# Splitting the last 96 rows of a weight matrix over two queues and both ends of a decode kernel

## The chip, the cores and the metric

One core of one Trainium2 chip. The metric is the device time of one execution in microseconds (us), as a median of several. Before: 659.82 us (3 runs, 659.73 to 659.85).

## The reference, cut to what matters

```python
h  = x  + attention(layernorm(x), k_cache, v_cache, wq, wo)   # B=2, one new token, 32 heads, 8192 keys, Dh=128
h2 = h  + (relu(ln @ W_gate) * (ln @ W_up)) @ W_down          # ln = layernorm(h), D=512, F=1376
```

K and V are 2 x 32 x 8192 x 128 bf16 each, 268 MB together. All else is small: wq and wo 4 MB each, the three matrices of the second part 1.4 MB each. W_down has 1376 = 10 x 128 + 96 rows; the last 96 rows, 1 KB each, are the subject.

## The kernel before

SyncE issues nearly every load. The start, and the places that matter at the end (cuts marked):

```python
nc.scalar.dma_start(x_row, A_x[:, 0]).then_inc(sem_x, 16)
nc.sync.dma_start(slot[3][:], A_wq.rearrange("(p c) n -> p (c n)", c=DC)).then_inc(sem_wq, 16)
nc.sync.dma_start(wo_rows, ...).then_inc(sem_wl, 16)
load(0, A_k_cache, 0); load(1, A_v_cache, 0); load(2, A_k_cache, 1)
# ... 32 pairs of K and V tiles of 4 MB through four slots ...
# last tiles in flight: the weights of the second part, into slot 0
for k, w in enumerate((B_W_up, B_W_gate)): nc.sync.dma_start(slot[0][...], w...)
for k, (r0, n) in enumerate(((0, 4), (4, 4), (8, 2))):              # three blocks of W_down
    nc.sync.dma_start(slot[0][...], B_W_down[r0 * 128:(r0 + n) * 128]...).then_inc(sem_wd[k], 16)
nc.sync.dma_start(wd_last[:], B_W_down[F - FR:]).then_inc(sem_wd[3], 16)   # FR = 96
# ... up product, gate product, hd = relu(gate) * up, then the down product:
order = [(f, k) for k, (r0, n) in enumerate(WD_BLOCKS) for f in range(r0, r0 + n)] + [(10, 3)]
for n, (f, k) in enumerate(order):
    pe.wait((sem_wd[k], 16))
    for m in range(4): nc.tensor.matmul(Op[0][...], lhsT=hd[...], rhs=...)
```

So the 96 rows are the last load issued and the last operand used.

The softmax here doesn't subtract the row's maximum and nothing guards it: scores larger than these inputs give would overflow.

## Time and profile before

| | before |
|---|---|
| median | 659.82 us |
| span in the profile | 658.6 us |
| DMA's part of the chain that ended last | 80% |
| bytes read | 281 MB, 427 GB/s over the span |
| PE's wait for wq ends | 12.98 us |
| third block of W_down complete | 656.09 us |
| the 96 rows complete | 656.29 us |

A load that is spread over all 16 DMA engines tells its arrival by 16 counts on a semaphore, one from each engine. The trace keeps the time of each, so a load has a first, a mean and a last arrival. The mean says how far the stream as a whole has come; the last says when a waiting engine may start. What PE waited for first:

```profile
12.98 0.10 PEld L256 LDWEIGHTS O<-slot,xlT 128*2 128x2 bf16 x8 [7.73 <-DMA slot<-in_A_wq_dram]
```

The brackets give the idle time before the instruction and what ended it: PE had been ready for 7.73 us, so wq's arrival sets the start of everything.

### The profile page before, as it was taken

Reading aid. Unit: us, or ns where it says so; the run is one execution under the profiler, and the core shown is the slowest. Engines: PE = TensorE matmul, PEld = TensorE weight load, DVE = VectorE, ACT = ScalarE, POOL = GpSimd, SP = SyncE. Lnnn points to the kernel's source line nnn. Section 1 sums busy time; section 2 is a strip of 40 time slices with the busy share of each in tenths; the row PEclk is TensorE's granted clock in tenths of the full one; section 3 lists DMA queues with packets and bytes.
Section 4 is the critical chain, followed back from the end, with each engine's and each line's share of the span. In section 5 each row is a group of like instructions: output and inputs, shape, how many; then the busy total and the mean of one; then the engine's idle time right before and its main releaser. Section 6 shows DMA issues by size and latency. Waiting matters only on the chain.

```text
span 658.6 us, 7569 instructions
## 1 busy us (share of the span) xinstructions
PE 326.1 (50%) x3066; PEld 192.1 (29%) x3067; DVE 469.4 (71%) x280; ACT 214.2 (33%) x433; POOL 72.7 (11%) x125
## 2 busy tenths in 40 slices
PE   2753444435554354644535453554445454454586
PEld 0431322214332132422213232322323222232354
DVE  1585576788767678776768867677876767787991
ACT  1622332243342233334223243323324322433151
POOL 3001002020200202020020201102020010202000
PEclk9999565565576555576655577555566755557567
DMA  8999999999999999999999999999999999999997
GB/s 366 445 426 437 426 442 418 442 420 444 424 436 438 422 440 420 444 422 438 430 432 438 422 440 420 444 422 438 440 422 436 424 438 424 440 428 436 434 415 307
DMA packets 10645, 281.17 MB, mean 427 GB/s; under 512 B 1190, under 2 KB 1292, under 8 KB 1804
## 3 DMA queue, kind: packets, MB, share of 16 engines
q1 hardware_dynamic: 10628, 281.06, 99.4%
q8 instruction: 5, 0.08, 0.0%
q14 instruction: 4, 0.03, 0.0%
q10 hardware_dynamic: 8, 0.00, 0.0%
HBM read 281.05 MB, written 0.00 MB: 427 GB/s over the span
## 4 chain that ended last, share of the span: by engine, by line
DMA 80%; DVE 18%; issue 1%; SPq 0%; DVEq 0%; PE 0%
DMA slot<-in_A_k_cache_dram 76%; DVE prod L539 16%; DMA slot<-in_B_W_down_dram 4%; DVE prod L548 2%; DVE scores L553 0%; SPq L171 0%; SPq L702 0%; SPq L698 0%; DVE kT L815 0%; DVEq L586 0%; PE O L807 0%; DVEq L590 0%; SPq L175 0%; SPq L174 0%; DVE zi L505 0%
## 5 line engine op out<-in xcount | busy, mean ns | idle before, releaser
L539 DVE TENSOR_TENSOR prod<-slot,q_c 128x12288 bf16<-128x12288 bf16 x32 | 209.9, 6558 | 148.1 <-DMA slot<-in_A_k_cache_dram 141.4
L404 PE MATMUL O<-slot,e 128*16 128x512 bf16 x1024 | 117.2, 609 | 219.3 <-ACT e L494 146.3
L548 DVE TENSOR_TENSOR prod<-prod 128x6144 bf16<-128x6144 bf16 (+3 forms) x128 | 212.3, 1658 | 7.8
L565 ACT ACTIVATE kT<-T 128x1024 bf16<-128x1024 bf16 x128 | 126.2, 1022 | 144.6 <-PE T L380 141.7
L380 PE MATMUL T<-ident_f,slot 128*128 128x128 f32 x512 | 112.8, 376 | 29.4 <-DVEq L586 29.4
L404 PEld LDWEIGHTS O<-slot,e 128*16 128x16 bf16 x1024 | 26.1, 112 | 284.6 <-ACT e L494 172.9
L494 ACT ACTIVATE e<-scores 64x96 bf16<-64x96 f32 x64 | 19.5, 304 | 239.8 <-DVEq L600 237.0
L380 PEld LDWEIGHTS T<-ident_f,slot 128*128 128x128 f32 x512 | 81.9, 193 | 44.4 <-DVEq L586 43.6
L536 POOL COPY q_c<-q_all 128x136 bf16<-128x136 bf16 x32 | 56.3, 1760 | 196.4 <-DVEq L590 152.5
L363 PE MATMUL S<-q_c,kT 128*128 128x4 bf16 x1024 | 47.6, 168 | 39.2 <-ACT kT L565 38.5
L363 PEld LDWEIGHTS S<-q_c,kT 128*128 128x128 bf16 x1024 | 39.6, 104 | 66.8 <-ACT kT L565 65.5
L416 PE MATMUL Ob<-sel,os_sb 128*128 128x4 f32 x136 | 31.0, 351 | 24.0 <-ACT os_sb L568 24.0
L416 PEld LDWEIGHTS Ob<-sel,os_sb 128*128 128x128 f32 x136 | 29.5, 319 | 25.9 <-ACT os_sb L568 25.9
L519 POOL MEMSET O_l<- 128x40 bf16 (+1 forms) x13 | 1.8, 136 | 303.9 <-DVEq L597 303.9
L553 DVE TENSOR_REDUCE scores<-prod 128x96 f32<-128x768 bf16 x32 | 30.5, 953 | 2.8
L565 ACT ACT_TABLE_LOAD x15 | 19.2, 1283 | 0.3
L494 ACT ACTIVATE e<-S 64x32 bf16<-64x32 f32 x64 | 13.0, 203 | 15.1 <-PE S L363 14.7
L568 ACT ACTIVATE os_sb<-O 128x512 f32<-128x512 f32 x17 | 10.2, 597 | 11.6 <-PE O L404 11.3
L494 ACT ACTIVATION_READ_ACCUMULATOR e<-S 64x1 f32 x64 | 12.8, 201 | 0.7
L494 ACT ACTIVATION_READ_ACCUMULATOR e<-scores 64x1 f32 x64 | 11.8, 184 | 0.0
L425 PEld LDWEIGHTS Ob<-zs,ones_f 128*128 128x128 f32 x30 | 7.1, 294 | 12.8 <-issue 12.8
L524 POOL COPY rsel<-rows 128x30 bf16<-128x30 bf16 x28 | 5.9, 209 | 33.3 <-DVEq L597 32.5
(104 smaller groups left out, 90.6 us busy)
## 6 DMA issues: line engine op xcount, KB each, us to landing
slot<-in_A_k_cache_dram SPq DMA_DIRECT2D x32, 4096.0 KB, 32.1
slot<-in_A_v_cache_dram SPq DMA_DIRECT2D x31, 4096.0 KB, 30.3
slot<-in_A_wq_dram SPq DMA_DIRECT2D x1, 4096.0 KB, 12.1
X<-in_A_wo_dram SPq DMA_DIRECT2D x1, 3840.0 KB, 46.0
slot<-in_A_v_cache_dram SPq DMA_DIRECT2D x1, 3072.0 KB, 23.1
slot<-in_B_W_up_dram SPq DMA_DIRECT2D x1, 1376.0 KB, 21.7
slot<-in_B_W_gate_dram SPq DMA_DIRECT2D x1, 1376.0 KB, 24.7
slot<-in_A_v_cache_dram SPq DMA_DIRECT2D x1, 1024.0 KB, 25.2
```

The lines of the kernel that those rows point to most:

```text
L363: i = nc.tensor.matmul(Sp[p % 2][:, 2 * jj:2 * jj + 4], lhsT=kv_[:, k, r, :], rhs=q_c[p % 2][:, 4 * r:4 * r + 4], start=(r == 0), stop=(r ...
L380: i = nc.tensor.transpose(Tp[g % 2][:, k * 128:(k + 1) * 128], k_t[:, j:j + 2, :].rearrange("p j d -> p (j d)").bitcast(F32), ident_f[:])
L404: i = nc.tensor.matmul(Op[0][c:c + 16, :], lhsT=e_t[q][:, j // VJ, :], rhs=v_t[:, j:j + VJ, :].rearrange("p j d -> p (j d)"), start=(q == ...
L416: i = nc.tensor.matmul(Ob[:, 0:4], lhsT=os_sb[:, jj * Dh:(jj + 1) * Dh], rhs=sel[:, 4 * jj:4 * jj + 4], start=(jj == 0), stop=(jj == VJ - 1))
L425: return nc.tensor.matmul(bank[:, ZC:ZC + 8], lhsT=ones_f[:], rhs=zs[:], start=True, stop=True)
L494: i = nc.scalar.activation(out=e_t[q][h, j0 // VJ:j1 // VJ, 8 * q:8 * q + 8].rearrange("p g (j a) -> p g j a", a=2)[:, :, :, a], in_=src(h ...
L536: nc.gpsimd.tensor_copy(out=q_c[p % 2][:], in_=q_all[:, p]).then_inc(g2d, 1)
L539: return nc.vector.tensor_tensor(out=prod[:, 0:JC, :], in0=tile((2 * p) % 4)[:, 0:JC, :], in1=q_c[p % 2][:, 8:QW].unsqueeze(1).broadcast_t ...
L548: run(nc.vector.tensor_tensor(out=prod[:, 0:JC, 0:w], in0=prod[:, 0:JC, 0:w], in1=prod[:, 0:JC, w:2 * w], op=ALU.add))
L553: return nc.vector.tensor_reduce(out=scores[p % PG][:, 0:JC], in_=prod[:, 0:JC, 0:8], axis=AX.X, op=ALU.add)
L565: to_pe(nc.scalar.activation(out=kT[gg % 2][:], in_=Tp[gg % 2][:].bitcast(BF16), func=ACT.Copy))
L568: to_pe(nc.scalar.activation(out=os_sb[:], in_=Op[0][:], func=ACT.Copy))
```

## The change

The intent, as I read it: take the 96 rows out of the last place of SyncE's queue, put 28 of them into the first microseconds, where the DMA engines are still idle, and let GpSimd's own queue bring the other 68 while PE works on gate.

```diff
+    WD_TAIL = ((68, 16), (84, 12), (0, 68))
+                def load_tail(eng, k):
+                    r0, n = WD_TAIL[k]
+                    eng.dma_start(
+                        wd_last[r0:r0 + n], B_W_down[F - FR + r0:F - FR + r0 + n]).then_inc(sem_wd[3 + k], 16)
                 nc.scalar.dma_start(x_row, A_x[:, 0]).then_inc(sem_x, 16)
+                load_tail(nc.sync, 0)
+                load_tail(nc.gpsimd, 1)
                 nc.sync.dma_start(slot[3][:], A_wq.rearrange("(p c) n -> p (c n)", c=DC)).then_inc(sem_wq, 16)
...
-                        nc.sync.dma_start(wd_last[:], B_W_down[F - FR:]).then_inc(sem_wd[3], 16)
...
                 t_u = ffn_in(Sp[1], wup, 0, FC)
+                pool.wait(t_u)
+                load_tail(nc.gpsimd, 2)
...
-                    pe.wait((sem_wd[k], 16))
+                    for j in range(k, k + 1 if k < 3 else 6):
+                        pe.wait((sem_wd[j], 16))
```

More of the change, by code (lines that the diff above doesn't have):

```diff
@@ L98, in bass_sequential_preLN__gqa_block_cached__glu_gated_reglu__decode_kernel @@
         sem_w = [S(f"w{i}") for i in range(2)]
-        sem_wd = [S(f"wd{i}") for i in range(4)]
+        sem_wd = [S(f"wd{i}") for i in range(6)]
         slot = [sb(f"slot{i}", [128, SLOT], BF16) for i in range(4)]
```

## The prediction

> **What bounds the kernel now.** I read the page's queue table and 40 slices first, then the chain that ended last, then the order of instructions at both ends, and last the single DMA packets and arrivals, because the change touches only transfers.
>
> ```profile
> DMA  8999999999999999999999999999999999999997
> q1 hardware_dynamic: 10628, 281.06, 99.4%
> DMA 80%; DVE 18%; issue 1%; SPq 0%; DVEq 0%; PE 0%
> ```
>
> The 16 DMA engines are busy in every slice; only the first and the last are below nine tenths. The 18% of DVE on the chain is bookkeeping: it multiplies the K tile it has just received while the next tiles are already flowing. In the middle of the chain one loop trip takes 38.9 us (519.60 to 558.46 us) and brings four loads of 4096 KB, 16.78 MB: 432 GB/s. The bytes do not change here, so the time is **when the stream starts, plus the bytes at that rate, plus how raggedly the 16 engines finish.** I therefore look at the two ends. The start, SyncE's issues in order of time:
>
> ```profile
> 0.81 0.40 SPq L174 DMA_DIRECT2D slot<-in_A_wq_dram  x1
> 1.27 0.42 SPq L175 DMA_DIRECT2D prod<-in_A_wo_dram  x1
> 1.73 0.42 SPq L171 DMA_DIRECT2D slot<-in_A_k_cache_dram  x1
> ```
>
> One issue follows the other every 0.46 us. Among the packets, wq's first one begins at 1.83 us, 1.02 us after its issue began. Before that the engines carry only x. The end, first the stretches (the last two figures are the share of 16 engines busy, and GB/s), then the chain and the instructions:
>
> ```profile
> 653.00:654.00 1.00, 1.00 (x37) 1.00 (x35) 0.00 (x0) 0.00 (x0) 0.00 (x0) 0.50 0.95 356
> 654.00:655.00 1.00, 0.64 (x20) 0.56 (x20) 0.18 (x1) 0.00 (x0) 0.00 (x0) 0.50 0.42 148
> 655.00:656.00 1.00, 0.94 (x32) 0.37 (x20) 0.00 (x0) 0.00 (x0) 0.00 (x0) 0.50 0.22 74
> ...
> 629.40 26.68 DMA slot<-in_B_W_down_dram
> 656.09 0.04 issue
> 656.13 0.52 PE O L807 x7
> ...
> 656.13 0.38 PE L807 MATMUL O<-slot,hd 128*2 128x128 bf16 x8 [0.20 <-DMA slot<-in_B_W_down_dram]
> 656.34 0.28 PE L807 MATMUL O<-wd_last,hd 96*2 96x128 bf16 x4
> ```
>
> From 654 us most engines have nothing left, yet the kernel waits until 656.09 us for the **third block of W_down**, not for the last 96 rows. The arrivals show why. The first W_down block reaches its 16 counts in three flocks: eight at 652.10 to 652.27, three at 652.66 to 652.79, five at 653.47 to 653.91. Five engines run 1.4 to 1.8 us behind the leaders. The lag is old: after the second V load one engine is already about 1 us behind, just after an instruction fetch (a packet of 16,384 B at 32.49 us, 1.06 us long) ran on one engine; another such fetch at 57.56 us puts a second one behind. Because the queue never runs dry, nobody catches up. The third block's last count comes at 656.09 us, the 96 rows' last at 656.29 us. PE needs from 656.13 to 656.34 us to issue the eight matmuls of the third block, and only then wants the 96 rows: **their wait is hidden to within hundredths of a microsecond.**
>
> **What the Trainium skill says.** "DMA: Bandwidth & Descriptors", section "Issuing engines are not separate DMA queues": all queues share the same 16 engines, so issuing from GpSimd buys no bandwidth, only issue time. This trace has no GpSimd data transfer to test that with; it does show the engines shared (the instruction fetches of another queue delay data). The same page, section "Why a DMA increments its semaphore by 16 and not by 1": a transfer uses the largest number of engines up to 16 that divides its rows, so 16 rows use 16, 12 use 12 and 68 use 4, taken on GpSimd in turn from a round-robin cursor; but it also tells of GpSimd transfers spread by ceil(rows/16) per engine, which for 68 rows is 5 rows on 13 engines and 3 on one. The trace agrees for 96 rows (16 counts arrive); no run before shows 12 or 68. The same page, "Anatomy of one DMA — SWDGE (gpsimd) path": about 2 us fixed for a GpSimd transfer. Nothing before shows it. "Runtime: NRT & Kernel Launch", section "Instruction fetch mechanics": instructions are refilled in 16 KiB blocks; the 16,384 B packets agree.
>
> **The change part by part.**
>
> 1. *Sixteen rows by SyncE ahead of wq.* The data is nothing: one row of 1 KB per engine, 46 ns a packet in this trace. But wq's issue moves one period back, from 0.81 to 1.27 us, so its first packet comes at about 2.29 instead of 1.83 us. The row occupies 0.05 us of that; the rest is an empty engine. wq itself has slack nowhere, since everything queues behind it: **+0.46 us**, and it persists through the loop, because DMA is the bound.
> 2. *Twelve rows by GpSimd at the start.* At one row per engine, 0.04 us on twelve engines, within wq's stream or in the gap before it: **+0.0 to +0.04**. Its issue also delays GpSimd's constants by an estimated 1 to 2 us. The transposes that need them ran at 4.9 us, and PE then waited for wq until 12.98 us, 7.6 us: hidden.
> 3. *The 96 rows leave the end of SyncE's queue.* That is 6 rows, 6 x 46 ns = 0.28 us on every engine, and one issue of 0.50 us that ran at 630.2 us with over 20 us of work queued: hidden. The 0.28 us lie behind the third block in each engine's ring, so the third block's arrival does not move. Gain: 656.34 minus the end of the eight issues, **0 to -0.05**.
> 4. *68 rows by GpSimd after the up product.* Up ended at about 651.7 us, later by part 1. Adding the skill's 2 us as an estimate, the rows would be there near 654 to 655 us if alone, before the third block at 656.5. They matter only if they sit on a lagging engine ahead of its third block. On four leading engines: 17 x 46 ns = 0.78 us inside 1.7 us of idleness, **0**. On fourteen engines: 5 x 46 ns on the laggards too, **+0.21 to +0.23**. On four engines with a laggard among them: up to **+0.75**.
> 5. *Two more waits on PE* before the last four matmuls: an issue step on the chain is 0.02 to 0.1 us, **+0.0 to +0.1**, mostly under the eight matmuls.
>
> Sum of parts 1, 2 and 3 with four leading engines: 659.82 + 0.46 + 0.04 - 0.03 = 660.3. With the fourteen-engine spread 660.5; with a laggard hit 661.0.
>
> **The rivals.** *The front is free.* The first wq packets took 1.4 to 2.2 us against 1.22 us later, and all end at 3.7 to 4.05 us whether they began at 1.83 or 2.64. Something at the start is common to all and need not be the issue; if the small transfer takes that start-up upon itself, wq may lose nothing. Against it: x's packets at 1.75 us took only 44 ns, so the engines were not cold, and a fill delay would recur after an idle gap. Time 659.7 to 659.9. *The laggards gain.* If the kernel waited for the 96 rows, 0.28 us would come off, which is surely the intent: rows placed on engines that stand idle, and balanced as 12 and 4. The arrivals speak against it (656.09 rules, not 656.29). Time 659.5 without a front loss, and 660.0 with one. *GpSimd's transfer is late.* If issue plus landing takes over 4.5 us, the last 68 rows take over from the third block as the last wait; the skill's 2 us speak against it, contention in a shared ring for it. Time 661 or more. *Instruction fetches move.* Added instructions shift the 16 KiB boundaries; one fetch more or fewer on a laggard is 1 us on that engine: +-0.3 at most on average.
>
> **Range and chances.** I weigh the full front cost at about 6 in 10, a partly or fully hidden front at 3 in 10, and a fourteen-engine or laggard hit on top at about 4 in 10. The middle is 660.2 us; 659.5 to 660.9 covers both the intent coming true and a moderate hit. A 2% change is 13 us; nothing here is a tenth of that except a wholly unexpected stall of GpSimd. So 0.004 for faster, 0.988 for the same, 0.008 for slower.
>
> **What would show each step.** Right: wq's issue at 1.27 and its first packet near 2.29 us; PE's wait for wq ends near 13.4 instead of 12.98; K and V arrivals all about 0.46 us later; one-row GpSimd packets near 2 to 3 us; at the end the third block still the last wait, near 656.5, and the 68 rows landed before it. Wrong: K arrivals unchanged against before (front free); the flocks of arrivals changed in size or lag (rows on laggards, or moved fetches); PE's last wait on the 96-row tile; a GpSimd transfer that takes many microseconds, or holds up the first transposes past 12.98 us.

## The result, and the profile after

660.42 us (6 runs, 660.32 to 660.58) against 659.84 us (6 runs, 659.65 to 660.08) in the same rounds: 0.58 us longer. The ratio is 1.0009, with a 95% interval of 0.9996 to 1.0022. Ratios are the mean time of one kernel's fast runs over that of the other's of the same rounds, so not quite the ratio of the medians that I quote. Every one of the six runs is slower than every one of the six before, and a second measurement, with other kernels beside it, gave 660.34 (5 runs) against 659.90 (9 runs), again without overlap. The half microsecond is real, and small.

The changed kernel's start, in order of time:

```profile
0.82 0.39 SPq L176 DMA_DIRECT2D wd_last<-in_B_W_down_dram  x1
1.26 0.41 SPq L182 DMA_DIRECT2D slot<-in_A_wq_dram  x1
1.32 0.66 POOL L176 DMA_DIRECT2D wd_last<-in_B_W_down_dram  x1 [0.81 <-POOLq L851]
...
6.14 0.40 PE L249 MATMUL T<-ident,kT 2*128 2x2 bf16 x8 [6.14 <-DVE kT L240]
...
13.76 0.10 PEld L264 LDWEIGHTS O<-slot,xlT 128*2 128x2 bf16 x8 [7.31 <-DMA slot<-in_A_wq_dram]
```

wq is issued at 1.26 instead of 0.81 us, and PE starts on it at 13.76 instead of 12.98 us. GpSimd's issue, 0.66 us, delays the constants and with them the transposes to 6.14 us; PE still waits 7.31 us for wq after that, so this part is hidden.

The end of the chain, then PE's last groups:

```profile
630.18 26.46 DMA slot<-in_B_W_down_dram
656.65 0.04 issue
656.69 0.56 PE O L817 x10
...
656.69 0.10 PEld L817 LDWEIGHTS O<-slot,hd 128*2 128x2 bf16 x8 [0.34 <-DMA slot<-in_B_W_down_dram]
656.92 0.12 PEld L817 LDWEIGHTS O<-wd_last,hd 96*2 96x2 bf16 x4
```

The last wait is again for the third block (656.65, before 656.09), and the last four weight loads follow with no idle time of their own. The end has the same shape as before and is 0.56 us later. The three small loads and what they took from issue to landing (last column, us):

```profile
wd_last<-in_B_W_down_dram POOLq DMA_DIRECT2D x1, 68.0 KB, 4.0
wd_last<-in_B_W_down_dram SPq DMA_DIRECT2D x1, 16.0 KB, 1.7
wd_last<-in_B_W_down_dram POOLq DMA_DIRECT2D x1, 12.0 KB, 7.5
```

GpSimd's 12 rows take 7.5 us, although each of the packets takes 46 ns. The single packets show how. The rows were issued at 1.32 us, but are served only at 6.60 to 6.95 us, when each engine has served three packets of wq, 32 KB each. From there on an engine serves one 1 KB row, then a packet of wq (1.213 us), then GpSimd's 4-byte count, then the next packet of wq. The Trainium skill says in "DMA: Bandwidth & Descriptors", section "Queues, rings and completion order", that an engine takes turns between queues, a packet at a time. This trace agrees from the row on; why three packets of wq pass before it is not shown.

**Where the time comes from, in arrivals (us):**

| kernel | wq first packet | wq mean | V tile at 615 us, mean | third block, mean | third block, last |
|---|---|---|---|---|---|
| before | 1.83 | 12.79 | 615.38 | 654.81 | 656.09 |
| before_again | 1.83 | 12.79 | 615.38 | 654.83 | 655.81 |
| after | 2.30 | 13.37 | 615.96 | 655.37 | 656.65 |
| after_again | 2.30 | 13.34 | 615.92 | 655.33 | 656.51 |

The mean is 0.55 to 0.58 us late at wq, the first large load, and 0.50 to 0.56 us late at the last one. **By the arrivals the whole loss is made before 14 us and carried nearly unchanged through 640 us of full DMA queue.** Note how well the mean repeats (12.79 and 12.79) while the last arrival moves by 0.28 us between two runs of one kernel. For effects of this size the mean is the better instrument. It has its own chance, though, once something stands ahead of wq: in the two runs of one kernel under 1 and 2 below, wq's mean is 13.14 and 13.30.

The packets split the loss into parts. By the bytes that the large packets had moved, the changed kernel (two profiles) was 0.47 and 0.44 us late as soon as the first megabyte was in, before any row of GpSimd was served: that is SyncE's transfer ahead of wq. GpSimd's rows add 0.04 us where they are served. Another 0.07 us comes between 14 and 45 us, where the 32 KB packets take slightly longer than before (the arrivals show this part already at wq). Packets are longer there in all six profiles in which rows of a second queue were served among wq's packets, and in none of the other eight. Why is open.

### The profile page after: what moved, and what is told of

The parts are those of the page before. It is cut to its first block, busy times and chain, and to the rows that moved or that the text cites. A ratio compares the mean times of both kernels' runs of the same rounds, so it can differ in the third digit from the quotient of the medians.

```text
span 659.2 us, 7572 instructions
## 1 busy us (share of the span) xinstructions
PE 329.5 (50%) x3066; PEld 195.2 (30%) x3067; DVE 469.2 (71%) x280; ACT 214.4 (33%) x433; POOL 74.7 (11%) x127
## 4 chain that ended last, share of the span: by engine, by line
DMA 80%; DVE 18%; SPq 1%; issue 1%; DVEq 0%; PE 0%
DMA slot<-in_A_k_cache_dram 76%; DVE prod L547 16%; DMA slot<-in_B_W_down_dram 4%; DVE prod L556 2%; DVE scores L561 0%; SPq L172 0%; SPq L710 0%; SPq L706 0%; DVE kT L825 0%; PE O L817 0%; DVEq L594 0%; DVEq L598 0%; SPq L183 0%; SPq L182 0%; SPq L176 0%
## 5 line engine op out<-in xcount | busy, mean ns | idle before, releaser
L388 PE MATMUL T<-ident_f,slot 128*128 128x128 f32 x512 | 116.7, 386 | 29.2 <-DVEq L594 29.2
L388 PEld LDWEIGHTS T<-ident_f,slot 128*128 128x128 f32 x512 | 84.3, 198 | 44.3 <-DVEq L594 43.4
L502 ACT ACTIVATE e<-S 64x32 bf16<-64x32 f32 x64 | 12.9, 202 | 15.2 <-PE S L371 14.8
L502 ACT ACTIVATION_READ_ACCUMULATOR e<-S 64x1 f32 x64 | 12.8, 201 | 0.7
L433 PEld LDWEIGHTS Ob<-zs,ones_f 128*128 128x128 f32 x30 | 7.3, 303 | 12.8 <-issue 12.8
```

The source lines that it names most:

```text
L388: i = nc.tensor.transpose(Tp[g % 2][:, k * 128:(k + 1) * 128], k_t[:, j:j + 2, :].rearrange("p j d -> p (j d)").bitcast(F32), ident_f[:])
L433: return nc.tensor.matmul(bank[:, ZC:ZC + 8], lhsT=ones_f[:], rhs=zs[:], start=True, stop=True)
L502: i = nc.scalar.activation(out=e_t[q][h, j0 // VJ:j1 // VJ, 8 * q:8 * q + 8].rearrange("p g (j a) -> p g j a", a=2)[:, :, :, a], in_=src(h ...
```

## The experiments

Theory: SyncE's issue ahead of wq leaves the DMA engines without work for one issue period, and a full queue never gives it back; the end is neutral. Rivals: GpSimd's transfers make the loss; bytes make it, or a one-off start-up cost, and not the issue; the end part gains or loses. Times are medians of five runs, each beside the kernel before on the same chip. The interval of every ratio is about plus or minus 0.0013, 0.9 us, and holds 1.0 in all of them, so the verdicts rest on the arrivals, and on the medians only as a check. Edits are shown against the changed kernel (in e6_all_behind against the kernel before), cut to the lines that matter; the table of pieces and the waits follow them.

**1. SyncE's front transfer alone** (e1_sync_front). The 16 rows ahead of wq stay; the other 80 go back to the end of SyncE's queue.

```diff
-                load_tail(nc.gpsimd, 1)
-                load_tail(nc.gpsimd, 2)          # and pool.wait(t_u)
+                        load_tail(nc.sync, 1)    # 80 rows, behind the third block
```

> Only the 16 rows by SyncE stand ahead of wq; the other 80 rows stay with SyncE at the end of its queue, GpSimd loads nothing. Theory (one SyncE issue ahead of wq leaves the engines empty for one issue period): the first wq packet at about 2.30 us, wq's first count at about 13.06 (before 12.59), time about 660.3. Rival (GpSimd's part makes the loss): the first wq packet at 2.30 costs nothing later, time 659.8. On the spread of the 16 wq counts: if SyncE's extra issue alone widens it, last minus first is near 0.62 as with the change; if GpSimd's rows did it, near 0.36 as before, and wq's last count is 13.41.

Measured: 660.40 us against 659.88 (ratio 1.0008). First wq packet at 2.28 us, wq's first count 12.88 (13.06 expected), mean 13.14, that is 0.35 later than before; the third block's mean 655.13, 0.32 later. The spread of wq's arrivals was 0.50 us, between the two figures expected, and decides nothing. The time is more than 0.32 us explains. The end shows why; the groups before the third block's use:

```profile
648.28 1.87 PE L423 MATMUL Ob<-sel,os_sb 128*128 128x4 f32 x8 [0.70 <-ACT os_sb L575]
...
655.83 1.24 PE L815 MATMUL O<-slot,hd 128*2 128x128 bf16 x40 [0.36 <-DVE hd L805]
```

Here the eight f32 matmuls took 1.87 us (1.05 us in the profile of before), since the granted clock fell to half at 645.2 us instead of 649.4, and the down product ran without a wait for DMA: PE's own work ended last, 0.3 us after what the third block (656.30) would have allowed. Is that part of this kernel, or chance?

**2. The same again** (f3_sync_again, no edit).

> The kernel with only SyncE's 16 rows ahead of wq, again. Its first profile ended 0.3 us later than its last arrival explains, because the granted TensorE clock fell to half at 645.2 us, before the transposed sums at 648 us, and PE and not DMA ended last. Theory (that fall is chance): the clock falls later here, PE waits for the third block again, the mean of wq's arrivals is 13.1 to 13.2, time 660.1 to 660.3. Rival (the fall belongs to this kernel): time 660.4 again with the fall near 645.

Measured: 660.24 us against 659.78 (ratio 1.0006). The clock fell at 650.6 us, and PE waited for the third block again:

```profile
630.11 26.47 DMA slot<-in_B_W_down_dram
656.58 0.04 issue
656.62 0.58 PE O L815 x11
```

So the early fall was chance; before_again shows it too, at 644.7 us. The mean of wq's arrivals was 13.30, 0.51 late, a little above what I expected. **SyncE's issue alone costs 0.35 to 0.51 us, most of the change's loss.**

**3. Two issues ahead of wq** (e4_two_issues).

```diff
+                load_tail(nc.sync, 3)            # a second piece of 16 rows; GpSimd's last piece: 52 rows
```

> As the change, but two transfers of 16 rows by SyncE ahead of wq (GpSimd's last piece shrinks to 52 rows). Theory (every issue ahead of wq costs one period of 0.46 us): first wq packet at about 2.76 us, first wq count near 13.54, time 660.9. Rival (the loss is bytes or a one-off start-up): time 660.4 to 660.5 as the change.

Measured: 660.79 us against 659.88 (ratio 1.0013). SyncE's issues:

```profile
0.82 0.85 SPq L176 DMA_DIRECT2D wd_last<-in_B_W_down_dram  x2
1.72 0.50 SPq L183 DMA_DIRECT2D slot<-in_A_wq_dram  x1
```

The first wq packet came at 2.84 us, the mean of wq at 13.82, which is 0.45 to 0.48 us later than in the two profiles of the changed kernel and 0.52 to 0.68 later than in the two with SyncE's transfer alone. A dose twice as large has about twice the effect; a start-up cost that is paid once falls. The time is a weaker witness: the clock fell at 645.8 us, as in e1_sync_front, and PE's own work ended last; the third block's mean was 655.77, 0.96 late.

One more thing changed here. The gap before wq is now long enough for GpSimd's 12 rows: their packets start at 2.67 to 2.80 us, before wq's first, and they land after 1.9 us instead of 7.5:

```profile
wd_last<-in_B_W_down_dram POOLq DMA_DIRECT2D x1, 12.0 KB, 1.9
```

What they cost there can't be told apart from the second issue: wq's first packet follows its issue by 1.12 us (1.02 before), and after it nothing more is lost, for the first packet is 1.01 us late and wq's mean 1.03.

**4. GpSimd's 12 rows at the start alone** (e2_pool_front).

```diff
-                load_tail(nc.sync, 0)
-                load_tail(nc.gpsimd, 2)          # and pool.wait(t_u); 84 rows by SyncE at the end
```

> Only the 12 rows by GpSimd at the very start; the other 84 rows stay with SyncE at the end of its queue. Theory (only SyncE's issue ahead of wq delays the stream): wq's issue stays at 0.81 us and its first packet at 1.83, time 659.8 to 660.0, although the GpSimd rows may land as late as 8 us. Rival (GpSimd's transfer at the start disturbs the stream): wq's first count later than 12.7 us, time 660.2 or more.

Measured: 659.96 us against 659.90 (ratio 1.0000). First wq packet 1.84 us. The mean of wq's arrivals was 12.94, 0.15 late, and the third block's 654.93, 0.12 late. Each engine spent 46 ns on a row and 9 to 18 ns on counts, so the data explain about 0.05; the longer packets between 14 and 45 us make another 0.07. Small, but three to four times what I had put down. wq's first count, 12.74, is just past the rival's 12.7; the time is the theory's.

**5. Two such transfers** (f2_two_pool).

```diff
-                load_tail(nc.sync, 0)
+                load_tail(nc.gpsimd, 0)          # rows 84 to 95
                 load_tail(nc.gpsimd, 1)          # rows 72 to 83; 72 rows by SyncE at the end
```

> Two GpSimd transfers of 12 rows at the start, none by SyncE ahead of wq; SyncE loads 72 rows at the end. With one such transfer the mean of wq's arrivals rose from 12.79 to 12.94. Theory (each GpSimd transfer costs the shared engines 0.15 to 0.2 us, several times its rows): mean 13.1 to 13.2, time 660.0 to 660.2. Rival (that 0.15 was chance of the start): mean 12.8 to 12.95, time 659.9.

Measured: 660.33 us against 659.78, the runs lying in two groups (659.92 and 659.97; 660.33, 660.42 and 660.45; ratio 1.0007). The mean of wq's arrivals was 13.07, 0.28 late, just below what the theory asked. That GpSimd's rows cost something when they cut into wq is not chance: wq's mean was 12.78 to 12.82 in all five profiles with nothing ahead of wq or within it, and 12.94 and more here and in the other two with such rows and SyncE's wq first. That the second transfer costs as much as the first is not shown: the step of 0.13 is no larger than the 0.16 between two runs of one kernel (1 and 2). The profiled run, 659.97, is of the lower group, so the trace does not tell what the upper group waited for.

**6. The 16 rows by ScalarE** (f1_act_front). The same bytes at the start, but SyncE issues wq first.

```diff
-                load_tail(nc.sync, 0)
+                load_tail(nc.scalar, 0)          # behind x; nothing by GpSimd, 80 rows by SyncE at the end
```

> The same 16 rows at the start, but issued by ScalarE behind x; SyncE issues wq first as before, and loads the other 80 rows at the end of its queue. Theory (the cost is SyncE's issue period, not the bytes): wq's first packet at 1.83 us, the mean of wq's 16 arrivals at 12.8 to 12.9 (before 12.79, SyncE in front 13.14), time 659.9. Rival (any transfer in the engines ahead of wq costs the start-up): mean near 13.14, time 660.2 or more.

Measured: 660.13 us against 659.78 (ratio 1.0004). wq's issue is back at 0.81 and its first packet at 1.84 us, so the issue period is saved:

```profile
0.81 0.40 SPq L181 DMA_DIRECT2D slot<-in_A_wq_dram  x1
...
1.40 0.33 ACTq L176 DMA_DIRECT2D wd_last<-in_B_W_down_dram  x1
```

The DMA view gives the rows 7.1 us from issue to landing, about as long as GpSimd's:

```profile
wd_last<-in_B_W_down_dram ACTq DMA_DIRECT2D x1, 16.0 KB, 7.1
```

And the mean of wq's arrivals is 13.07, 0.28 late. A miss: I had expected 12.8 to 12.9. The rows now cut into wq's stream; its rows were served at 6.1 to 6.8 us, and of the 24 packets of 32 KB that start between 6.5 and 8.1 us 22 took 1.23 to 1.29 us instead of 1.213. Up to 14 us these longer packets add up to 0.13 us per engine. Why one row per engine lengthens the packets beside it stays open. What follows: handing the rows to another queue trades the idle gap for a disturbance of about half to four fifths of its size (0.28 against 0.35 to 0.51).

**7. Both small loads behind wq** (e5_behind).

```diff
-                load_tail(nc.sync, 0)
-                load_tail(nc.gpsimd, 1)
...
                 load(2, A_k_cache, 1)
+                load_tail(nc.sync, 0)
...
                 t_const = pool.run(nc.gpsimd.memset(zs[:], 0.0))
+                load_tail(nc.gpsimd, 1)
```

> As the change, but both small loads of the start are issued behind wq, the wo rows and the first three tiles. Theory (only the place ahead of wq costs): wq's first packet back at 1.83 us, wq lands as before at 12.94, and with the end part's small gain the time is 659.6 to 659.8. Rival (small GpSimd transfers cost wherever they stand): 660.2 to 660.4.

Measured: 660.03 us against 659.88 (one of the five at 661.06, which lifts the ratio to 1.0006). First wq packet 1.83 us; the mean of wq 12.97, 0.18 late, much as in e2_pool_front; the third block's mean 655.07, 0.26 late. "Behind wq" held for SyncE's rows only: GpSimd's, in a queue of their own, were served at 9.70 to 10.18 us, still among wq's packets. The 0.46 us of the issue are gone, the small gain that I expected of the end did not appear, and the time lies between the two expectations.

**8. GpSimd's 68 rows at the end alone** (e3_pool_end).

```diff
-                load_tail(nc.sync, 0)
-                load_tail(nc.gpsimd, 1)
+                        load_tail(nc.sync, 0)    # 28 rows, behind the third block
```

> Only the 68 rows by GpSimd after the up product; the other 28 rows stay with SyncE behind the third block. Theory (the end part gains a little because fewer 1 KB rows trail, and the front is untouched): wq lands as before at 12.94 us, the third block's last count 3.20 us after gate's last (before 3.45), time 659.6. Rival of the prediction (rows of GpSimd on lagging engines push the third block out by five rows of 46 ns): third block 3.6 to 3.7 us after gate, time 660.05.

Measured: 660.12 us against 659.88 (ratio 1.0004). wq's mean 12.78 and the third block's 654.80: the stream is exactly that of before, and GpSimd's rows do not push the third block. But they land last, at 656.34 against 655.93 us, and PE now waits for them:

```profile
655.98 0.10 PEld L816 LDWEIGHTS O<-slot,hd 128*2 128x2 bf16 x8 [0.29 <-DMA slot<-in_B_W_down_dram]
656.44 0.12 PEld L816 LDWEIGHTS O<-wd_last,hd 96*2 96x2 bf16 x4 [0.37 <-DMA wd_last<-in_B_W_down_dram]
```

The last product starts 0.14 us later than before (656.48 against 656.34). Neither gain nor the push that I had feared: a new wait, of a tenth of a microsecond. (The profiled run, 659.94, is the fastest of the five.)

**9. All 96 rows behind the first tiles** (e6_all_behind). No GpSimd, nothing ahead of wq, nothing at the end.

```diff
                 load(2, A_k_cache, 1)
+                nc.sync.dma_start(wd_last[:], B_W_down[F - FR:]).then_inc(sem_wd[3], 16)
...
-                        nc.sync.dma_start(wd_last[:], B_W_down[F - FR:]).then_inc(sem_wd[3], 16)
```

> All 96 rows by SyncE in one transfer, behind the first three tiles: nothing ahead of wq, nothing behind the third block, no GpSimd transfer. Theory (the 96 rows' wait was hidden at the end and their bytes are the same anywhere): within 0.15 us of the kernel before, 659.7 to 660.0; PE's last four matmuls follow the eight of the third block without a wait. Rival (the rows at the end cost 0.28 us on the last engine): 659.5 to 659.6.

Measured: 660.15 us against 659.90 (ratio 1.0003), slower by 0.25: both expectations missed. wq's mean is as before (12.82), the third block's is 0.51 us late. I had forgotten that **the very end of SyncE's queue is the one place, of those tried, where these rows are free**: there they lie behind the third block and pass under PE's eight matmuls. Here they stand ahead of it in each engine's queue, at 6 x 46 ns = 0.28 us. The packets show the rest: beside the rows, from 41.2 to 44.5 us, 36 packets of 32 KB took 1.25 to 1.49 us, in sum 0.3 us per engine. Why is open. (The profiled run, 660.29, is the slowest of the five.) The last product did follow without a wait.

**10. Which engines lag** (e7_probe). The prediction rests on five engines that run late. Here the 96 rows are cut into 64, 12, 8, 6, 4 and 2.

> The kernel before with the 96 rows cut into transfers of 64, 12, 8, 6, 4 and 2 rows, each with its own semaphore. If a transfer of n rows uses n engines and always the same lowest ones, the counts of the small ones show which engines lag: the five that are 1.4 us and more late are among the first eight (then the transfer of 8 rows shows up to five late counts) or not (then all eight come early). No time is read from it, about 660.

Measured (one look): the small transfers showed exactly 12, 8, 6, 4 and 2 data counts, besides one record each at the issue. Neither expectation held. Of the eight in the 8-row transfer two came early, three about 0.6 us later, and three 1.3 to 1.8 us later. If these are always the same lowest engines, as the Trainium skill states ("DMA: Bandwidth & Descriptors", section "Why a DMA increments its semaphore by 16 and not by 1"), three of the five laggards are among the first eight and the rest above: no split by halves would spare them, so I tried none.

On the lag's origin there is a test by accident, from the arrivals of the first V tile. In the profile of before, an instruction fetch of 16,384 B ran at 32.49 us, and one engine's share of the load then landing was 1.6 us behind the other fifteen. In e3_pool_end that fetch ran only at 33.72 us, when the same load was complete (33.15 us): all sixteen arrived within 0.55 us, and the straggler appeared one load later. f2_two_pool repeats it (fetch at 33.83, load complete at 33.68, no straggler); in the other twelve profiles the fetch ran before the load was complete, and one engine was late. That agrees with the fetch as the cause of this first straggler; where the other four laggards come from is not shown.

**11. and 12. Repeats** (after_again and before_again).

> The changed kernel a second time, beside the others on one chip. Expected 660.4 again, first wq packet again at 2.30 us. The spread of wq's 16 counts was 0.63 us the first time, 0.36 in the kernel before and 0.57 in a run whose start equals the kernel before: if that is chance, it is another number between 0.35 and 0.85 here and the time does not follow it; if the change makes it, it is 0.6 again.

Measured: 660.34 us against 659.90; first packet 2.30; wq's mean 13.34; the spread of wq's arrivals 0.56 us.

> The kernel before, profiled a second time, for the size of chance: the mean of wq's arrivals 12.79 within 0.05, of the third block's 654.81 within 0.05; the spread of wq's arrivals may differ (0.36 the first time).

Measured: 12.79 and 654.83 us, both inside the margins; the spread of wq's arrivals was 0.66 us instead of 0.36. The spread is chance, then, and not of the change. No variant beats the kernel before.

## Why the prediction was right

The time, 660.42 us, is 0.2 above the predicted 660.2 and inside the range; the sum of its own parts, 660.3, was nearer, and its case with fourteen engines, 660.5, nearer still, but that case is right partly by luck, as part 4 shows.

- *Part 1, SyncE's issue, +0.46 us:* right. The first wq packet was foretold at 2.29 us and came at 2.30. In the changed kernel's packets it is worth 0.44 to 0.47 us. Alone, the issue delayed the stream's mean by 0.35 and 0.51 us; a second one by 0.45 to 0.68 more, depending on the run it is compared with. That it persists to the end is shown by the table of arrivals.
- *Part 2, GpSimd's 12 rows, 0 to +0.04 us:* **mis-sized.** It measured +0.15 alone and +0.28 for two. I had counted rows times packet time. That is right for the place where the rows cut in (0.04 us), but it leaves out that packets after them take longer (0.07 us). The hiding of GpSimd's delayed constants was right.
- *Part 3, the rows leave the end, 0 to -0.05 us:* right in that they were hidden there. e6_all_behind shows the other side: behind the first tiles they cost 0.25 us.
- *Part 4, the 68 rows:* the spread over fourteen engines, one of my three cases, is what the packets show (thirteen joined packets of four rows with a fifth row behind each, and one share of three rows). The push of +0.21 us on the third block that I attached to it did not come: in e3_pool_end the block's mean was 654.80 against 654.81. Issue to landing took 4.0 us, twice the 2 us that I took from the skill, which makes these rows a new last wait in e3_pool_end; in the changed kernel they land at 656.81 us, after the third block (656.65) and not before it as foretold, but before PE loads them at 656.92. So the 660.5 of this case added a push of 0.21 us that did not come, and left out about 0.1 us of part 2.
- *Part 5, two more waits:* from the first use of the third block to the first matmul of the last rows 0.26 us (0.30 in after_again), before 0.21: +0.05 to +0.09, inside the range, though no run tries the waits alone.
- *The rivals:* "the front is free" falls by e1, f3 and e4; "the laggards gain" by e3 and e6. "GpSimd is late" holds in a small way. "Fetches move" was not needed.
- *The signs:* wq's issue at 1.27, its first packet at 2.29, late K and V tiles and the third block as the last wait came true. PE's wait for wq ended at 13.76 (13.58 in after_again), not near 13.4; GpSimd's rows were served at 6.6 to 7.0 us, not at 2 to 3, and their 7.5 us are one of the signs that I had listed as wrong.
- *The readings:* two slips that do not bear on the result. The first straggler, about 1.6 us late, is there with the first V load, not the second. And the lag is old for two engines only: until 615 us two are over 1 us late, five not before 652 us.

Right in its main step, then, and in the rest by errors that partly offset each other: part 2 was too small by about 0.1 us, the push of part 4 did not come, and the middle had been pulled down by the chance that the front is free.

## What to carry to other kernels

When the DMA queue is full from the first load to the last, the first large load must be issued first: one small issue ahead of it costs an issue period for good (here about 0.46 us), however few its bytes. Before moving a load off the end, see whether anything waits for it there; behind the last load that something does wait for, it may already be free. Judge changes of a tenth of a percent by the mean arrival of the engines' shares and not by the last one, which wanders.

## What the Trainium skill lacked or had wrong

- "DMA: Bandwidth & Descriptors", section "Anatomy of one DMA — SWDGE (gpsimd) path", gives about 2 us fixed for a GpSimd transfer. Where the 12 rows met idle engines that fits (1.9 us in e4_two_issues). The section does not say what a full stream adds: there it was 7.5 us (12 rows at the start) and 4.0 us (68 rows at the end). Nor is it GpSimd's alone: ScalarE's 16 rows took 7.1 us.
- The same page, section "Issuing engines are not separate DMA queues", says that issuing from several engines saves only issue time, usually small relative to the DMA. In this kernel that issue time, 0.46 us ahead of the first large load, is most of the effect, and the other queue was not neutral: one GpSimd transfer of 12 rows set the stream back by 0.15 us, one of ScalarE of 16 rows by 0.28 us. I found no page with that price.
- The same page, section "Queues, rings and completion order", does not say how long a second queue waits for its first turn: in five profiles exactly three 32 KB packets of wq per engine passed before its first row.
- The same page, section "Why a DMA increments its semaphore by 16 and not by 1", leaves open which GpSimd transfers are spread by ceil(rows/16) per engine (it says some): here 68 and 52 rows both were, five and four rows to an engine. Its rule for SyncE agrees with the runs: 84 and 72 rows gave 14 and 12 data counts.
- "Runtime: NRT & Kernel Launch", section "Instruction fetch mechanics", calls the cost of crossing a 16 KiB boundary mostly hidden, and names no cost to data. Here a 16 KiB fetch holds one of the engines that also carry the data for about 1 us, and with a queue that never runs dry the engine that was busy with it then stays late: the last arrivals are still 1.8 us behind the first at 61 us and at 615 us.
